# The first half of the first K by the sync queue in fp32, the other half by GpSimd with a cast

## The chip, the cores and the metric

The kernel runs on one core of a Trainium2 chip. The metric is the device time of one execution in microseconds (us). The span of a profile is about 1.85 us shorter than the time of the same execution (before: 424.3 for 426.1). In the profile lines below PE is TensorE (PEld its weight loads), DVE is VectorE, ACT is ScalarE, POOL is GpSimd and SP is the sync engine; a q after the name means its queue. `rk`, `rq` and `rv` are the tiles in SBUF that K, Q and V are loaded to, and `wt` is a place for weights.

## The reference, cut to what matters

Windowed attention over 8 batches, 8 heads, 576 positions, 64 channels; then a Fourier transform along the sequence, 64 modes each multiplied by a complex 512 x 512 weight, the inverse transform, and a residual with a relu layer.

```python
scores = scale * np.matmul(q, k.transpose(0, 1, 3, 2))     # masked to 0 <= i - j < 64, softmax
x = (attn @ v).transpose(0, 2, 1, 3).reshape(B, S, H * D)
X = np.fft.rfft(x, axis=1)
Yr = einsum('bmd,mde->bme', Xr, w_r) - einsum('bmd,mde->bme', Xi, w_i)   # 64 modes
...
return u + np.maximum(u @ w_ch, 0.0)                          # u = x + irfft(Y)
```

The two weight tensors are 64 x 512 x 512 fp32 each, 134 MB together. That is most of what is read.

## The kernel before: the parts that matter

All inputs of the first part and all weights but one (`w_ch`) come by DMAs that GpSimd issues and that cast fp32 to bf16 on the way. Each K, Q or V of one batch is one DMA of 128 partitions x 2 halves x 1152 elements: 1.18 MB read, 0.59 MB written.

```python
    WP = [wlate.tile([128, 2, NC, DM], BF16, name="wt", tag=f"wp{j}") for j in range(LW // 2)]
    ...
    def load(b, which):
        r = raw_tile(which)
        nc.gpsimd.dma_start(
            out=r, in_=RAW[which][b].rearrange("(x g) (p c) d -> (g p) x (c d)", g=4, c=RUN))
        raws[b, which] = r
    ...
    nc.vector.memset(warm, 0.0)
    load(0, "k")
    load(0, "q")
    ...                      # identity; then the tables of the transform (VectorE, ScalarE)
    load(0, "v")
    ...                      # band mask (GpSimd)
    for which in "kqv":
        load(1, which)
```

The places `WP` are for weights that arrive much later; at the start they are empty.

The softmax here doesn't subtract the row's maximum and nothing guards it: scores larger than these inputs give would overflow.

## Time and profile before

| | before |
|---|---|
| median of 3 runs | 425.99 us (425.98 to 426.3) |
| profiled span | 424.3 us |
| busy: PE, VectorE, ScalarE, GpSimd | 82%, 44%, 40%, 19% |
| written by all DMAs | 91.98 MB |
| first packet of the first load | 2.78 us |
| last weight lands | 389.34 us |

PE's 82% looks like the bound, but it is a mean over stages with different limits. What decides is the row of DMA shares by slice, and the end of the chain of waits; the prediction below shows both. A cast load reads two bytes for each byte that it writes, so a row of 213 GB/s written is 426 GB/s read. An uncast fp32 load at full rate shows about 400 to 420 GB/s written. Bear this in mind for every table of stretches.

I use one derived number throughout, the **effective start**: 10 us minus the time that the bytes of the first 10 us need at full rate. At 213 GB/s it is 3.52 us for the kernel before. For bytes that came uncast, half are counted.

### The profile page before, as it was taken

Reading aid. Unit: us, or ns where it says so; the run is one execution under the profiler, and the core shown is the slowest. Engines: PE = TensorE matmul, PEld = TensorE weight load, DVE = VectorE, ACT = ScalarE, POOL = GpSimd, SP = SyncE. Lnnn points to the kernel's source line nnn. Section 1 sums busy time; section 2 is a strip of 40 time slices with the busy share of each in tenths; the row PEclk is TensorE's granted clock in tenths of the full one; section 3 lists DMA queues with packets and bytes.
Section 4 is the critical chain, followed back from the end, with each engine's and each line's share of the span. In section 5 each row is a group of like instructions: output and inputs, shape, how many; then the busy total and the mean of one; then the engine's idle time right before and its main releaser. Section 6 shows DMA issues by size and latency. Waiting matters only on the chain.

```text
span 424.3 us, 8778 instructions
## 1 busy us (share of the span) xinstructions
PE 348.6 (82%) x3762; PEld 217.9 (51%) x3772; DVE 184.6 (44%) x397; ACT 171.3 (40%) x314; POOL 78.9 (19%) x141
## 2 busy tenths in 40 slices
PE   6989998998998899364698977977568986589993
PEld 4655765665665465122365644555234442266782
DVE  5566765766663201061443413332113432140994
ACT  4585765866863311021132312122213332130992
POOL 7231231331121131212111011212121132200000
PEclk9999999999995699755699999999899999979998
DMA  8999999999999999999999999999999999994598
GB/s 143 211 213 213 211 214 213 212 214 211 216 212 215 214 215 263 214 215 214 214 215 214 214 215 214 214 215 213 215 212 214 213 214 214 214 214 92 197 385 328
DMA packets 27782, 91.98 MB, mean 217 GB/s; under 512 B 2352, under 2 KB 2608, under 8 KB 27616
## 3 DMA queue, kind: packets, MB, share of 16 engines
q0 software_dynamic: 24480, 81.80, 96.4%
q1 hardware_dynamic: 3120, 9.50, 5.9%
q8 instruction: 29, 0.48, 0.4%
q10 hardware_dynamic: 144, 0.13, 0.1%
q14 instruction: 9, 0.07, 0.0%
HBM read 162.53 MB, written 9.44 MB: 405 GB/s over the span
## 4 chain that ended last, share of the span: by engine, by line
DMA 44%; PE 36%; DVE 8%; issue 7%; ACT 2%; POOL 1%; DVEq 0%; POOLq 0%
DMA wt<-in_moe_w_r_dram 27%; DMA wt<-in_moe_w_i_dram 17%; PE pso L324 7%; PE pst L226 6%; PE psy L592 5%; PE pso L905 4%; PE psv L243 3%; DVE x_sb L332 3%; PE psx L346 3%; PE pss L381 2%; PE pss L280 2%; PE pss L299 2%; DVE vT L59 2%; DVE ot L928 1%; PE pso L790 1%
## 5 line engine op out<-in xcount | busy, mean ns | idle before, releaser
L592 PE MATMUL psy<-wt,XQ 128*32 128x512 bf16 (+1 forms) x404 | 85.0, 428 | 42.9 <-DMA wt<-in_moe_w_i_dram 27.0
L592 PEld LDWEIGHTS <-XQ 128*32 128x32 bf16 (+1 forms) x476 | 46.8, 133 | 82.3 <-issue 64.9
L621 DVE CAST xT<-pxt 128x256 fp32r<-128x256 bf16 (+1 forms) x68 | 26.0, 435 | 56.3 <-PE pxt L614 40.3
L628 ACT CAST Z<-psz 128x512 fp32r<-128x512 f32 x36 | 21.2, 588 | 58.4 <-PE psz L626 58.1
L305 ACT ACTIVATE et<-pss 128x512 bf16<-128x512 f32 x72 | 39.2, 599 | 13.4 <-PE pss L299 13.4
L626 PE MATMUL psz<-wch,xT 128*128 128x512 f32 x144 | 39.5, 410 | 0.4 <-DVE xT L621 0.4
L324 PE MATMUL pso<-vt,et 128*64 128x65 bf16 (+1 forms) x576 | 34.3, 210 | 4.8 <-DVE x_sb L332 4.7
L324 PEld LDWEIGHTS <-et 128*64 128x64 bf16 (+1 forms) x576 | 24.0, 114 | 17.1 <-issue 9.5
L626 PEld LDWEIGHTS psz<-wch,xT 128*128 128x128 f32 x144 | 25.5, 188 | 11.2 <-issue 5.4
L59 DVE COPY x_sb<-psy 128x256 f32<-128x256 f32 x15 | 6.4, 424 | 53.6 <-PE psy L592 53.5
L58 ACT COPY x_sb<-psy 128x256 f32<-128x256 f32 x15 | 5.6, 374 | 57.8 <-DVE x_sb L59 57.8
L332 DVE TENSOR_TENSOR x_sb<-pso,rcp 128x640 bf16<-128x640 f32 x32 | 26.3, 823 | 0.9
L122 POOL DMA_DIRECT2D wt<-in_moe_w_r_dram x15 | 10.7, 715 | 75.5 <-PE psy L592 68.0
L905 PE MATMUL pso<-Y,trigI 128*128 128x512 f32 x80 | 23.1, 403 | 0.1
L928 DVE TENSOR_TENSOR ot<-pso,x_sb 128x512 f32<-128x512 f32 x35 | 22.2, 685 | 1.5 <-PE pso L905 1.1
L280 PE MATMUL pss<-band,ident_bf 64*64 64x512 bf16 x136 | 20.7, 414 | 1.5 <-ACT et L305 1.5
L59 DVE COPY vT<-pst 128x768 bf16<-128x768 bf16 x16 | 15.3, 958 | 13.0 <-PE pst L226 13.0
L59 DVE CAST x_sb<-psj 128x512 bf16<-128x512 f32 x18 | 12.2, 688 | 19.8 <-PE psj L807 16.6
L117 POOL DMA_DIRECT2D wt<-in_moe_w_r_dram x25 | 13.6, 544 | 35.9 <-PE psy L592 17.2
L910 ACT ACTIVATE pso<-pso 128x512 f32<-128x512 f32 x36 | 19.1, 594 | 0.0
L58 ACT CAST x_sb<-psj 128x512 bf16<-128x512 f32 x18 | 10.6, 586 | 20.5 <-PE psj L807 20.5
L117 POOL DMA_DIRECT2D wt<-in_moe_w_i_dram x21 | 11.4, 542 | 34.1 <-PE psy L592 18.8
(159 smaller groups left out, 533.6 us busy)
## 6 DMA issues: line engine op xcount, KB each, us to landing
wt<-in_moe_w_r_dram POOLq DMA_DIRECT2D x15, 1024.0 KB, 23.0
wt<-in_moe_w_i_dram POOLq DMA_DIRECT2D x15, 1024.0 KB, 25.4
wt<-in_moe_w_r_dram POOLq DMA_DIRECT2D x25, 512.0 KB, 18.0
wt<-in_moe_w_i_dram POOLq DMA_DIRECT2D x21, 512.0 KB, 17.9
out_dram<-ot SPq DMA_DIRECT2D x15, 512.0 KB, 4.3
rk<-in_k_dram POOLq DMA_DIRECT2D x8, 576.0 KB, 9.8
rq<-in_q_dram POOLq DMA_DIRECT2D x8, 576.0 KB, 13.7
rv<-in_v_dram POOLq DMA_DIRECT2D x8, 576.0 KB, 12.4
```

What stands on the lines that cost most here:

```text
L59: return nc.vector.tensor_copy(out=o, in_=i)
L117: nc.gpsimd.dma_start(out=wt, in_=src[m].rearrange("(p c) e -> p c e", c=NC))
L226: nc.tensor.transpose(out=ps[64 * hh:64 * hh + 64, c, :], in_=src[:, hh, (c0 + c) * D:(c0 + c + 1) * D], identity=ident_bf)
L280: nc.tensor.matmul(out=pss[(2 * w + hh) % 3][64 * half:64 * half + 64, :], lhsT=ident_bf[pp, pp], rhs=view(band[pp], 128 * half, [[0, WIN ...
L305: nc.scalar.activation(out=et[:, hh, :], in_=pss[(2 * w + hh) % 3], func=ACT_F.Exp, scale=EX_SCALE)
L324: nc.tensor.matmul(out=pso[po, hh, (i // 2) * VW:(i // 2) * VW + D + 1], lhsT=et[pk, hh, col:col + 64], rhs=vt[pk, 1 - f % 2, 2 * hh + g / ...
L332: nc.vector.tensor_tensor(out=view(x_sb, b * NT * DM + g * D, [[4 * D, 2], [DM, NT], [1, D]]), in0=view(pso, 0, [[512, 2], [VW, NT], [1, D]]),
L592: nc.tensor.matmul(out=psy[r0:r0 + k, :], lhsT=xq(c, m, im, [[NM, k]]), rhs=w[:, c, :], start=(im + c == 0), stop=(im == (m > 0) and c == ...
L621: nc.vector.tensor_copy(out=xT[:, :, w * k:w * k + w], in_=view(psts[k], j, [[128, NC], [n, w]] if n > 1 else [[128, NC], [1, 64], [64, 2]]))
L626: nc.tensor.matmul(out=psz, lhsT=xT[:, c, :], rhs=wch[:, c, :], start=(c == 0), stop=(c == NC - 1))
L905: nc.tensor.matmul(out=tps[n], lhsT=trigI[:, tr:tr + 128], rhs=pair_tile(what, bb), start=False, stop=stop and r0 + k == 128, skip_group_c ...
L928: nc.vector.tensor_tensor(out=ot[:, j], in0=ps, in1=x_sb[:, b, t, :], op=ALU.add)
```

## The change

Its intent is to start the stream of loads earlier: the sync queue has nothing to do before its first DMA (it issues at 0.74 us in the profile after, GpSimd at 1.24). Its half comes without a cast, so it lands in fp32 in an empty weight place, and VectorE casts it.

```diff
     def load(b, which):
         r = raw_tile(which)
-        nc.gpsimd.dma_start(
-            out=r, in_=RAW[which][b].rearrange("(x g) (p c) d -> (g p) x (c d)", g=4, c=RUN))
+        src = RAW[which][b].rearrange("(x g) (p c) d -> (g p) x (c d)", g=4, c=RUN)
         raws[b, which] = r
+        if (b, which) != (0, "k"):
+            nc.gpsimd.dma_start(out=r, in_=src)
+            return
+        wide = view(WP[0], 0, [[1, 2 * RUN * D]]).bitcast(FP32)
+        nc.sync.dma_start(out=wide, in_=src[:, 0])
+        nc.gpsimd.dma_start(out=r[:, 1], in_=src[:, 1])
+        nc.vector.tensor_copy(out=r[:, 0], in_=wide)
```

## The prediction

> **What bounds the kernel now.** I began with the page's 40 slices, because the load, the arithmetic and the store of this kernel overlap and a mean over the span hides which one ends last.
>
> ```profile
> PE   6989998998998899364698977977568986589993
> DMA  8999999999999999999999999999999999994598
> GB/s 143 211 213 213 211 214 213 212 214 211 216 212 215 214 215 263 214 215 214 214 215 214 214 215 214 214 215 213 215 212 214 213 214 214 214 214 92 197 385 328
> ```
>
> One slice is 10.6 us. From the second to the 36th slice the DMA row is a 9 and the rate stays near 213 GB/s (one slice is higher because it carries the one weight that isn't cast to bf16). PE has slices of 3, 4 and 6 in the same time. Only the first slice is short of bytes (143 GB/s). So the loads form one long stream, and what is left after it is the tail in which the result is computed and stored.
>
> The chain that ended last, read at the end of the stream, says the same:
>
> ```profile
> 351.10 18.58 DMA wt<-in_moe_w_i_dram
> ...
> 371.48 17.87 DMA wt<-in_moe_w_i_dram
> 389.34 0.05 issue
> 389.39 0.72 PE psl L796 x16
> ```
>
> The last weight, 512 KB, is issued at 371.48 us and lands at 389.34. At 213 GB/s its own bytes need 0.52 MB / 213 GB/s = 2.5 us, so it spends about 15 us behind earlier loads. The queue is never empty there; GpSimd issues early enough. After the landing follows a tail of 424.3 - 389.3 = 35 us of PE, VectorE and stores that depends on that landing. So the span is: start of the stream, plus its bytes over its rate, plus a fixed tail.
>
> The start of the stream is in the table of stretches (the columns are the stretch, its length, busy time of PE, PEld, DVE, ACT, POOL, then clock, DMA share, GB/s) and in GpSimd's own timeline:
>
> ```profile
> 2.00:2.50 0.50, 0.00 (x0) 0.00 (x0) 0.50 (x1) 0.50 (x1) 0.50 (x2) 1.00 0.00 0
> 2.50:3.00 0.50, 0.00 (x0) 0.00 (x0) 0.07 (x1) 0.00 (x1) 0.50 (x2) 1.00 1.20 65
> 3.00:3.50 0.50, 0.00 (x0) 0.00 (x0) 0.00 (x0) 0.00 (x0) 0.41 (x3) 1.00 0.42 28
> 3.50:4.00 0.50, 0.11 (x1) 0.11 (x1) 0.33 (x2) 0.35 (x2) 0.50 (x3) 1.00 0.81 138
> 4.00:4.50 0.50, 0.50 (x2) 0.41 (x3) 0.49 (x3) 0.50 (x1) 0.49 (x2) 1.00 1.08 207
> ```
> ```profile
> 1.25 0.83 POOL L99 DMA_DIRECT2D rk<-in_k_dram  x1 [0.80 <-POOLq L971]
> 2.07 0.73 POOL L99 DMA_DIRECT2D rq<-in_q_dram  x1
> ```
>
> The first K is issued at 1.25 us, and no byte moves before 2.5 us; a finer look puts the first packet at 2.78, that is 1.5 us after the issue began. Full rate is there from 4.0 us. The first 14 packets alone have a share of 1.196 of 16 engines in half a microsecond: 1.196 x 16 x 0.5 / 14 = 0.68 us each, against about 0.19 us later (1.093 x 16 x 1.0 / 91). So the stream pays a slow first packet on each engine. Over the first 10 us it moved 1.38 MB; at 212 GB/s that is 6.5 us of full rate, so the stream behaves as if it started at full rate at **3.5 us**. That number is all the change can work on, if the above is right.
>
> The arithmetic at the start does not wait for K. The first K lands 5.6 us after its issue, at about 6.85, while PE is in 14 warm-up matmuls until 9.37 and starts the transposes of K at 9.3. So an earlier K by itself starts nothing earlier.
>
> **What the Trainium skill says.** "DMA: Bandwidth & Descriptors", section "Latency and other measured facts", gives a first byte after some 600 ns for the hardware path (sync, scalar) and some 1 us for GpSimd's path. The trace shows longer ones, and a smaller gap: 1.5 us for the first K on GpSimd; on the sync queue, in the tail, a 32 KB transfer issued at 395.35 has its first packet at 396.75 (1.4 us), and the first store, issued at 396.22, starts moving in bulk at about 397.42 (1.2 us). I use 1.2 to 1.4. The same page, section "Issuing engines are not separate DMA queues", says that concurrent issue from several engines saves only the issue time, since all run on the same 16 engines. No view of the kernel before tests that; it is why I count no extra bandwidth. The section "SWDGE vs HWDGE vs iDMA" says that a cast in the DMA is for GpSimd only: hence the fp32 place and VectorE's cast. "VectorE: DVE Perf Modes", section "The perf-mode tier table", has an fp32 copy within SBUF run at two elements a cycle; the trace agrees in slope: the TENSOR_SCALAR of 128x384 fp32 takes 0.36 us and that of 128x256 0.29, so 0.55 ns an element.
>
> **The change part by part.**
>
> *Bytes.* Half of one K goes as fp32 to fp32: 128 x 1152 x 4 = 0.59 MB written in place of 0.29. Does that lengthen the stream? The cast loads write 213 GB/s and so read 426. The stretch 160 to 200 us moved 227 GB/s on average, with the uncast 1.05 MB weight in it: (227 - 214) x 40 us = 0.52 MB more than usual, exactly half of 1.05. So an uncast load writes twice as fast as a cast one, and the engines are limited by what they read. Half a K takes 0.59 / 426 = 1.38 us either way. Cost 0.
>
> *The start.* The sync queue has nothing to do before its first DMA; its only early wait is 0.7 us for the start of the program, and VectorE, released by the same, begins at 0.87. So I put sync's issue at 0.85 and its first packet at 0.85 + 1.2 to 1.4 = 2.05 to 2.25, against 2.78. That is 0.5 to 0.7 us earlier. The slow first packets (0.68 us) then still come, but 0.29 MB x 2 of sync's data, 1.38 us of work, covers the time in which GpSimd's own first packets are slow (2.78 to 3.6), so this loss is paid once and earlier. Effective start about 2.15 + 0.6 = 2.75 in place of 3.5: **a gain of 0.75 us**, from 0.5 to 1.0.
>
> *GpSimd.* Its first issue has 128 rows in place of 256. Loads of 128 rows take it 0.53 to 0.57 us, those of 256 rows 0.70 to 0.83, so about 0.2 us less. The second issue and the identity that PE's warm-up waits for come 0.2 us earlier. PE's warm-up start (3.89) could move by that; it isn't on the path of the stream.
>
> *VectorE.* The cast of 1152 fp32 elements costs 0.36 + 768 x 0.55 ns = 0.78 us. It waits for the sync load, which I expect to land at about 2.15 + 0.6 + 1.4 + 0.5 = 4.6 us. VectorE is in order: between 3.63 and 8.35 it makes the identity and the tables. A wait plus the cast may push the tables' end from 8.35 by 1 to 2 us, and ScalarE's two table steps (8.39 to 8.9) with it, past 9.86, where ScalarE evacuates the first transposes. So PE's attention may begin up to 1 us later. Does it reach the end? Only if the load queue runs dry. Its smallest reserve that I find is at 23.95, where six loads of the first two batches and three more have been issued: 9 x 0.59 MB / 212 GB/s = 25 us from 3.5, so until 28.5: 4.5 us of reserve. 0.75 us earlier and 1 us later still leave 2.8. No cost.
>
> *The weight place* is next written by a load issued at 24.66, long after the cast. No cost.
>
> Sum: -0.75 + 0 + 0 = -0.75 us, that is 425.99 to **425.3** rounded, with the tail unchanged.
>
> **The rivals.** (1) *Hidden anyway*: the sync queue's first packet comes no earlier than GpSimd's, because its first use at the start of a program is slower than in the tail; then the time stays at 426.0. Against it: two tail issues show 1.2 and 1.4 us. For it: no sync DMA is issued early in the trace before, so its start-up is not seen. (2) *VectorE becomes a wait at the start*: the cast stalls the tables, PE starts 1 to 2 us later. If PE set the time in the attention part this would give 427; the load queue's unbroken 213 GB/s speaks against it. (3) *PE sets the attention part and its earlier start by 0.2 us counts too*: 425.0. PE is over 90% busy from 20 to 120 us, which speaks for it, but the weights of the later part must still come through the full stream. (4) *Fp32 packets disturb the cast ones*, both queues sharing 16 engines: some tenths back, 425.7.
>
> **Range and chances.** Rivals 1 and 4 set the upper side, 426.1 with the noise of 0.3 us in the three runs before; an issue at 0.7 and an earlier full rate set the lower side, 424.6. Two per cent is 8.5 us; the whole idle start of the stream is 3.5 us, so faster by that is out of reach, and slower would need the load queue to run dry or an order of instructions that the scheduler spoils later.
>
> **What would show it.** Right: first packet on the sync queue near 2.1, full rate by about 3 us, 10 us mark with some 0.16 MB (bf16 measure) more than before, the last weight landing near 388.6 in place of 389.34, the tail still 35 us. The cast should take about 0.8 us. Wrong: a start of packets at 2.7 or later (rival 1), gaps in the load rate between 20 and 50 us (rival 2), a last landing earlier without an earlier start (rival 3), or a tail of another length, which would be an order or clock effect that I did not foresee.

## The result, and the profile after

| | before | changed |
|---|---|---|
| median, 4 runs each side by side | 426.14 us (425.98 to 426.6) | 426.76 us (426.64 to 427.03) |
| profiled span | 424.3 | 424.8 |
| effective start | 3.52 | 3.78 |
| last weight lands | 389.34 | 389.59 |
| landing to end of span | 35.0 | 35.2 |

The ratio is 1.0014, with an interval from 0.9996 to 1.0031: the same within 2%. The median is above the predicted range and the forecast gain is absent; that the kernel became slower is not clear of the noise, as the interval includes 1.

The page of the changed kernel, by slices of the span, still shows one unbroken stream:

```profile
PE   6999998999988897364598978878569897588993
DMA  8999999999999999999999999999999999994598
GB/s 165 212 212 212 214 214 211 214 212 212 214 214 213 213 214 263 214 214 214 214 215 213 215 215 215 212 215 215 213 214 213 214 214 213 214 212 88 211 378 320
```

Its first slice has 165 GB/s for 143 before, which looks like a gain of 15%. It is not one: the sync half counts double there. Over the first 10 us the changed kernel wrote 162 GB/s, so 1.62 MB. Less half of the uncast 0.59 MB that is 1.325 MB, or 6.22 us of full rate. The effective start is 10 - 6.22 = 3.78 us, 0.26 us **later** than before.

The end of the chain of waits says the same: the last weight lands 0.25 us later than before, and the tail after it goes once through a small load that the kernel before does not have on its chain (the first columns are start and length in us):

```profile
371.30 18.29 DMA wt<-in_moe_w_i_dram
389.59 0.05 issue
389.63 0.73 PE psl L802 x16
...
407.06 4.20 DMA Y<-yl
```

What the two added instructions did is in the timeline (start, length, engine, line, operation, and in brackets the idle time before it and what ended it):

```profile
0.74 0.39 SPq L105 DMA_DIRECT2D wt<-in_k_dram  x1
1.24 0.66 POOL L106 DMA_DIRECT2D rk<-in_k_dram  x1 [0.79 <-POOLq L977]
1.89 0.73 POOL L102 DMA_DIRECT2D rq<-in_q_dram  x1
4.28 0.84 DVE L107 CAST rk<-wt 128x1152 bf16<-128x1152 f32 x1 [1.71 <-DMA wt<-in_k_dram]
9.06 0.42 DVE L159 TENSOR_TENSOR gff<-gff,mtf 128x256 f32<-128x256 f32 x1
```

Sync issues at 0.74, and its first packet starts at 1.77 us, 1.01 us before the first packet of a load in the kernel before. The cast takes 0.84 us; the last step of the tables ends at 9.48 in place of 8.35. So the change does what it was meant to. At 4.0 us the changed kernel has 1.67 us of full rate behind it, the kernel before 0.54: **1.13 us ahead**, counted from the packets.

The loss comes right after. The table of stretches of the changed kernel (stretch, length, busy PE, PEld, DVE, ACT, POOL, clock, DMA share, GB/s):

```profile
2.50:3.00 0.50, 0.00 (x0) 0.00 (x0) 0.07 (x1) 0.00 (x1) 0.48 (x3) 1.00 0.96 350
3.00:3.50 0.50, 0.00 (x0) 0.00 (x0) 0.00 (x0) 0.05 (x1) 0.43 (x4) 1.00 1.04 383
3.50:4.00 0.50, 0.29 (x1) 0.29 (x2) 0.00 (x0) 0.48 (x2) 0.50 (x2) 1.00 0.99 189
4.00:5.00 1.00, 1.00 (x3) 0.82 (x3) 0.72 (x1) 0.96 (x1) 0.99 (x3) 1.00 0.94 141
5.00:6.00 1.00, 1.00 (x4) 0.73 (x3) 0.95 (x6) 0.00 (x0) 0.94 (x5) 1.00 1.01 67
6.00:7.00 1.00, 1.00 (x4) 0.82 (x3) 0.93 (x5) 0.00 (x0) 1.00 (x4) 1.00 0.76 138
7.00:8.00 1.00, 1.00 (x5) 0.86 (x4) 0.97 (x4) 0.51 (x2) 1.00 (x3) 1.00 1.12 212
```

and of the kernel before in the last four of these:

```profile
4.00:5.00 1.00, 1.00 (x3) 0.82 (x4) 0.99 (x5) 1.00 (x1) 0.99 (x4) 1.00 1.09 210
5.00:6.00 1.00, 1.00 (x4) 0.81 (x3) 0.93 (x4) 0.14 (x1) 0.94 (x3) 1.00 1.10 210
6.00:7.00 1.00, 1.00 (x3) 0.76 (x3) 0.49 (x4) 0.62 (x2) 1.00 (x5) 1.00 1.11 210
7.00:8.00 1.00, 1.00 (x4) 0.77 (x3) 0.92 (x5) 0.00 (x0) 1.00 (x2) 1.00 1.13 217
```

From 4 to 8 us the changed kernel wrote 141 + 67 + 138 + 212 = 558 KB of cast data, which is 2.62 us of full rate in 4 us: it **lost 1.38 us** there, the kernel before 0.03. The DMA share (a packet counts whole where it begins) is near 1 even where only 67 GB/s moved, so the packets there are slow rather than missing: of the packets that began between 5 and 6 us, 14 took over 0.4 us, up to 1.9 us, where 0.19 us is usual. In order of start they are among the 90th to the 122nd of GpSimd's packets. Its half of K has 128, so they lie about where the 16 engines pass from K to Q; which load each one belongs to the trace does not say. I call this the hole. It turns the lead of 1.13 us at 4 us into an arrears of 0.26 us at 10 us, which then stays (0.27 at 380 us).

### The profile page after: what moved, and what is told of

It is laid out like the page before. It is cut to its first block, busy times and chain, and to the rows that moved or that the text cites. A ratio compares the mean times of both kernels' runs of the same rounds, so it can differ in the third digit from the quotient of the medians.

```text
span 424.8 us, 8781 instructions
## 1 busy us (share of the span) xinstructions
PE 347.7 (82%) x3762; PEld 216.9 (51%) x3772; DVE 185.4 (44%) x398; ACT 171.2 (40%) x314; POOL 78.8 (19%) x141
## 4 chain that ended last, share of the span: by engine, by line
DMA 37%; PE 36%; issue 12%; DVE 9%; POOL 2%; ACT 2%; POOLq 0%; DVEq 0%; SPq 0%
DMA wt<-in_moe_w_r_dram 23%; DMA wt<-in_moe_w_i_dram 14%; PE pso L330 7%; PE pst L232 6%; PE psy L598 4%; PE psv L249 3%; DVE x_sb L338 3%; PE psw L751 3%; PE pso L911 3%; PE pss L387 2%; PE pss L286 2%; PE psx L352 2%; DVE ot L934 2%; PE pss L305 2%; DVE vT L59 2%
## 5 line engine op out<-in xcount | busy, mean ns | idle before, releaser
L598 PE MATMUL psy<-wt,XQ 128*32 128x512 bf16 (+1 forms) x404 | 86.1, 426 | 42.9 <-DMA wt<-in_moe_w_i_dram 26.0
```

The source lines that it names most:

```text
L598: nc.tensor.matmul(out=psy[r0:r0 + k, :], lhsT=xq(c, m, im, [[NM, k]]), rhs=w[:, c, :], start=(im + c == 0), stop=(im == (m > 0) and c == ...
```

## The experiments

Each is measured by the same three numbers: the loss in 4 to 8 us, the lead over the kernel before at 10 us (how much earlier the effective start is), and the landing of the last weight. The rows are grouped as the argument goes. Each row is one profile; two pairs of the same kernel show how far two profiles differ: 1.38 and 1.11 lost (changed and e13), 0.37 and 0.21 (e6 and e12).

| run | GpSimd's first packet, us | sync's last packet ends | loss 4-8 us | lead at 10 us | last weight lands |
|---|---|---|---|---|---|
| before | 2.78 | - | 0.03 | 0 | 389.34 |
| changed | 3.42 | 3.91 | 1.38 | -0.26 | 389.59 |
| e13 (changed, again) | 3.27 | 3.88 | 1.11 | -0.09 | (1) |
| e1 no cast | 3.40 | 3.89 | 1.31 | -0.18 | 389.9 |
| e5 cast late | 3.38 | 3.82 | 0.97 | +0.24 | 389.7 |
| e7 no cast, no tables | 3.31 | 3.75 | 0.94 | +0.10 | (2) |
| e4 whole K + unread sync half | 3.48 | 3.92 | 1.43 | -0.44 | 391.8 |
| e3 two halves, GpSimd only | 2.58 | - | 0.88 | -0.38 | 389.9 |
| e8 Q in halves, GpSimd only | 2.79 | - | 0.07 | +0.07 | 389.1 |
| e10 Q issued later | 3.56 | 4.01 | 0.77 | +0.28 | 389.5 |
| e11 half K, Q, half K, GpSimd | 2.60 | - | 0.29 | +0.08 | (2) |
| e9 Q first on GpSimd | 3.59 | 4.07 | 0.48 | +0.48 | 388.9 |
| e14 sync reads V | 3.62 | 4.29 | 1.07 | -0.17 | 390.0 |
| e15 as e4, sync reads V | 3.98 | 4.37 | 1.17 | -0.34 | 391.9 |
| e18 sync half in two transfers | 3.23 | 6.33 | 0.57 | +0.24 | (2) |
| e6 K by sync | 4.70 | 5.10 | 0.37 | +1.12 | 388.3 |
| e12 K by sync, again | 4.99 | 5.41 | 0.21 | +1.02 | 388.7 |
| e16 Q by sync | 4.98 | 5.54 | 0.30 | +1.03 | 388.5 |
| e19 Q by sync, V early | 5.00 | 5.41 | 0.20 | +1.08 | 388.3 |
| e17 changed + second sync load | 5.11 | 5.66 | 0.05 | +1.00 | (1) |

In e4, e15 and e17 the lead counts bytes that nobody reads, worth 1.38 us; without them e17 is 0.38 us behind. (1) In these profiles the granted clock was 0.911 and 0.915, and PE, not the load, closed the chain; see e13. (2) e7, e11 and e18 lost 2 to 5 us of stream between 100 and 380 us for a reason that I did not find; only their first 10 us are used.

### Is it VectorE's cast, or its late tables? e1, e5, e7

The first theory was a lock. The Trainium skill, page "SBUF — State Buffer", section "SBUF: two separate sides", says that an fp32 copy within SBUF on VectorE shuts GpSimd out of a shared pair of ports, so that GpSimd can't write the descriptors of its DMAs. The trace of the changed kernel has such a sign: a band step on GpSimd took 0.78 us beside the cast (from 4.43 us), the same step in the kernel before 0.26.

e1 removes the cast (the half is set to zero; a wrong K):

```diff
-        nc.vector.tensor_copy(out=r[:, 0], in_=wide)
+        nc.vector.memset(r[:, 0], 0.0)
```

> Wrong on purpose: half of the first K is zeros set at the start, the sync load into the weight place stays, the VectorE cast is gone. Theory A (the cast is what breaks the load stream between 4 and 7 us, by shutting GpSimd out while it runs): the rate from 4 to 7 us goes back to about 210 GB/s from 141, 67 and 138; some 1 us more of the stream is done by 10 us; last weight lands near 388.4 to 388.7; time 425.2 to 425.6. Theory B (GpSimd's queue pays its slow first packets again because it starts behind the sync queue's packets, cast or not): the hole stays, 425.9 to 426.9.

Measured: 426.93 us, ratio 1.0017 [1.0005, 1.0029]. The hole is there without the cast:

```profile
4.00:5.00 1.00, 1.00 (x3) 0.82 (x3) 0.96 (x5) 0.95 (x1) 0.99 (x5) 1.00 1.06 152
5.00:6.00 1.00, 1.00 (x4) 0.73 (x3) 0.96 (x4) 0.15 (x1) 0.94 (x3) 1.00 1.09 74
6.00:7.00 1.00, 1.00 (x4) 0.82 (x3) 0.47 (x3) 0.47 (x2) 1.00 (x4) 1.00 0.81 145
```

e5 keeps the cast but holds it back until the tables are done:

```diff
-        nc.vector.tensor_copy(out=r[:, 0], in_=wide)
+        casts.append(lambda: nc.vector.tensor_copy(out=r[:, 0], in_=wide))
...                                  # VectorE's order held as written
+    casts.pop()()                   # after gen_trig
```

> As the changed kernel, with the cast held back on VectorE until after the tables (about 8.4 us instead of 4.3). A: the hole between 4 and 7 us is gone; if the cast as such does the harm, a hole shows up after 8.4 us instead, and if it only hurts while descriptors of the first loads are being fetched, none does; 425.2 to 425.7 in the second case. B: hole at 4 to 7 us as in the changed kernel, 426 to 427. The first K transposes start near 9.2 to 9.5 in both.

Measured: 427.42 us, ratio 1.0021 [1.0009, 1.0033]; 88 GB/s in 5 to 6 us, loss 0.97.

e7 takes away the cast and the tables (wrong, relative error 0.027):

```diff
-        for t0, t1 in ((0, 3), (3, NT)):
-            ...
-            gen_trig(tmp, mt, n * NM, ...)
+        nc.vector.memset(trigF, 0.0)
```

> Wrong on purpose: as e1_no_cast, and VectorE's and ScalarE's cosine and sine tables are replaced by zeros set at the start, so VectorE does almost nothing between 3 and 9 us. Theory Q (VectorE's fp32 work in that time keeps GpSimd from writing the descriptors of the loads that it has already issued): no hole at 5 to 6 us, rate near 210 GB/s, about 1 us more moved by 10 us than in e1_no_cast. P and R: the hole stays as in e1_no_cast, 74 GB/s from 5 to 6 us.

Measured: one look, 429.33 us at a clock of 0.905, so the time says nothing. VectorE was busy for 0.65 us of the 4 us in question, and the loss was still 0.94 us. What follows: the cast did cost GpSimd half a microsecond of its own work, but neither the cast nor VectorE's tables make the hole. Its size varies by some tenths between executions (e13 below: 1.11 for 1.38), so the differences among 0.94, 0.97 and 1.31 are not read. A second sign comes from e17 below: there the same cast ran beside a band step of 0.85 us, and there was no hole. e5 also shows how loosely the start and the time hang together: 0.24 us ahead at 10 us, its last weight landed 0.3 us late.

### Is it the sync queue, or the halves? e3, e4, e8

e3 does without sync and without a cast: two GpSimd loads of 128 rows.

```diff
-        nc.sync.dma_start(out=wide, in_=src[:, 0])
+        nc.gpsimd.dma_start(out=r[:, 0], in_=src[:, 0])
         nc.gpsimd.dma_start(out=r[:, 1], in_=src[:, 1])
-        nc.vector.tensor_copy(out=r[:, 0], in_=wide)
```

> No sync load and no cast: GpSimd loads the two halves of the first K as two DMAs of 128 rows. A and B: stream like the kernel before (full rate from 4 us, no hole), 426.0 plus or minus 0.3. Rival C (a load of half a K, 128 rows, is itself what starts slowly): packets of 0.5 us and more after the first ones, and a hole as in the changed kernel, 426.5 or more.

Measured: 426.37 us, ratio 1.0005 [0.9992, 1.0019]. A loss of 0.88 us, mostly at 6 to 7 us (99 GB/s). The two halves have 256 packets, and the slow ones (0.7 us and more) are mostly the 262nd to the 285th, where Q begins. So a hole of this kind needs no sync load.

e4 leaves GpSimd's loads as before and adds the sync load, which nobody reads:

```diff
-        nc.gpsimd.dma_start(out=r[:, 1], in_=src[:, 1])
-        nc.vector.tensor_copy(out=r[:, 0], in_=wide)
+        nc.gpsimd.dma_start(out=r, in_=src)
```

> GpSimd loads the whole first K as before, and the sync queue loads half of it once more into the weight place, where nobody reads it; no cast. 0.59 MB more to read, 1.38 us at 426 GB/s. A: no hole; the stream starts 1.1 us earlier and carries 1.4 us more, so about +0.3 us against before, 426.2 to 426.6. B: hole behind the sync packets, another 1 us on top, 427.0 to 427.6.

Measured: 428.85 us, ratio 1.0061 [1.0049, 1.0073]; loss 1.43, last weight at 391.8. So the hole does not need the halves either: a sync load beside the unchanged GpSimd loads is enough. Of the 2.45 us by which the last weight came later, 1.38 are the extra bytes. Nor is the hole tied to the start of Q: the packets of 0.9 us and more in e4 are among the 50th to the 85th of the 256 of the whole K.

e8 is the kernel before with the first Q, not K, in two GpSimd loads:

```diff
+        if (b, which) != (0, "q"):
+            nc.gpsimd.dma_start(out=r, in_=src)
+            return
+        for x in range(2):
+            nc.gpsimd.dma_start(out=r[:, x], in_=src[:, x])
```

> The kernel before with Q, not K, loaded as two GpSimd DMAs of 128 rows; K whole as before. P and Q: engines come to Q at 6.2 us, more than 3 us after its issue, so no slow packets, full rate as before. C (a load of 128 rows makes the load after it start slowly, as the halves of K did in e3_halves_gpsimd): first packets of 1 us at the start of the second half of Q or of V, a hole of some tenths between 7.5 and 10 us.

Measured: one look, 426.13 us, no hole (loss 0.07). Loads of 128 rows as such are harmless. Its span also goes through the wait for `yl` in the tail, so that wait needs no sync load.

### Is it the time between GpSimd's issue and its first packets? e9, e10, e11

Another theory (P in the expectations) was that a GpSimd load is not ready until some microseconds after its issue, and that Q was wanted too soon. e9 issues Q ahead of the half K, e10 issues Q after the small constants (at 2.74 us in place of 1.89), and e11 uses GpSimd only, with half K, Q, half K.

```diff
e9:  -        nc.gpsimd.dma_start(out=r[:, 1], in_=src[:, 1])
     +        casts.append(lambda: nc.gpsimd.dma_start(out=r[:, 1], in_=src[:, 1]))
      ...     load(0, "q")
     +    casts.pop()()
e10: -    load(0, "q")             # after load(0, "k")
     +    load(0, "q")             # just before load(0, "v")
e11: -        nc.sync.dma_start(out=wide, in_=src[:, 0])
     -        nc.gpsimd.dma_start(out=r[:, 1], in_=src[:, 1])
     -        nc.vector.tensor_copy(out=r[:, 0], in_=wide)
     +        nc.gpsimd.dma_start(out=r[:, 0], in_=src[:, 0])
     +        casts.append(lambda: nc.gpsimd.dma_start(out=r[:, 1], in_=src[:, 1]))
      ...     load(0, "q")
     +    casts.pop()()
```

> The changed kernel with GpSimd issuing Q before its half of K, all else the same. P: engines come to Q at 3.5 us, 1.5 us after its issue ended, so they are slow there as the first packets of the kernel before are (0.6 to 1.1 us each), then the half of K is long ready: a loss of about 0.5 in place of 1.3 us, about 0.5 us ahead of before at 10 us, 425.5 to 425.9. R: as the changed kernel or e4_extra_sync, slow packets from 4 to 7 us, 426.5 to 427.

> The changed kernel with one line moved: GpSimd issues Q after its small constants, ending at about 3.3 us in place of 2.6; the engines still finish the half of K at about 5.0. P (the engines wait at Q because its load was issued too short a time ago): the slow first packets of Q last 0.7 us longer, to about 6.5 to 7.8 us instead of 5.8 to 7.1, and some 0.5 us less has been moved by 8 us than in the changed kernel (4.28 us' worth there, about 3.8 here). If the hole ends at a fixed time or belongs to the order of loads, it stays at 4.3 us' worth by 8 us.

> GpSimd alone, no sync load, no cast: half of K, then Q, then the other half of K. The engines come to Q at about 4.4 us, some 1.9 us after its issue ended. P: first packets of Q of 1 us and more from 4.4 us on, ending near 6 us, and none when the engines come to the second half of K near 8 us. If a start behind another queue or the cast were needed for slow packets, none here.

Measured: e9 427.52 us, ratio 1.0016 [0.9987, 1.0045], with a profile that is 0.48 us ahead and whose last weight lands at 388.9; its timed runs scatter from 425.97 to 428.19 and don't confirm a gain. e10 one look, 426.55; its loss is smaller (0.77, spread as 168, 164, 180 and 177 GB/s over the four microseconds), though Q had less time. e11 one look, 430.12 (see (2) above), loss 0.29, with Q in use 1.9 us after its issue. The profile of e9 came out as P said (0.48 lost, 0.48 ahead), those of e10 and e11 against it: less time did not hurt. A comparison of e15 and e16 (below) speaks against it too. In both GpSimd issues the whole K at 1.25 us; among K's packets that began between 6 and 7 us, nine took 0.4 to 0.88 us in e15, and none over 0.31 us in e16. A fixed time from issue to readiness does not give that, so this theory falls.

### All of the first K by sync: e6, e12

```diff
-        nc.sync.dma_start(out=wide, in_=src[:, 0])
-        nc.gpsimd.dma_start(out=r[:, 1], in_=src[:, 1])
-        nc.vector.tensor_copy(out=r[:, 0], in_=wide)
+        for x in range(2):
+            wide = view(WP[x], 0, [[1, 2 * RUN * D]]).bitcast(FP32)
+            nc.sync.dma_start(out=wide, in_=src[:, x])
+            nc.vector.tensor_copy(out=r[:, x], in_=wide)
```

> The whole first K by the sync queue in fp32 into two weight places, two VectorE casts; GpSimd begins with Q at 1.25 us, so Q's load has been issued 3.4 us before the engines can come to it (about 4.6). Theory P (a GpSimd load issued at the start is not ready for the DMA engines until some 3 to 4 us after its issue ended, and engines that come to it sooner have first packets of 1 us and more): no hole, 1.1 us ahead of before at 10 us, 425.0 to 425.5. Theory R (packets of GpSimd's queue are slow whenever they follow those of the sync queue): slow packets from 4.6 on, no gain left, 426 to 427.

> e6_k_by_sync once more, beside the changed kernel on the same chip, for the time: 1.1 us ahead by 10 us as before, last weight near 388.3; 0.6 us faster than before and 1.2 us faster than the changed kernel if the gain of the stream reaches the end, equal to before if it doesn't.

Measured: 425.38 us, ratio 0.9979 [0.995, 1.0008], and again, on another chip, 425.51 us, ratio 0.9981 [0.9965, 0.9996]. At 10 us the stream is 1.12 and 1.02 us ahead; its last weight lands 1.1 and 0.6 us earlier. The medians are 0.60 and 0.56 us under the kernel before, though e6's interval still includes 1. This is what the prediction wanted to see, with two halves in place of one. The rates of e12, the smaller lead of the two, show no such hole:

```profile
4.00:5.00 1.00, 1.00 (x3) 0.77 (x3) 0.61 (x1) 0.41 (x1) 0.94 (x4) 1.00 1.07 419
5.00:6.00 1.00, 1.00 (x4) 0.79 (x3) 0.38 (x2) 0.00 (x0) 1.00 (x5) 1.00 1.04 189
6.00:7.00 1.00, 1.00 (x4) 0.82 (x3) 0.95 (x4) 0.00 (x0) 1.00 (x2) 1.00 1.10 207
7.00:8.00 1.00, 1.00 (x3) 0.76 (x3) 0.97 (x5) 0.00 (x0) 1.00 (x2) 1.00 1.12 210
```

e13 is the changed kernel once more, on the chip of e12 (no edit):

> The changed kernel itself, once more: does the hole come back with the same size (rates near 141, 67, 138 GB/s from 4 to 7 us, 0.2 to 0.3 us behind before at 10 us), and is the time again 0.4 to 0.7 us over before? If the hole is a chance of one profile, the rates differ.

Measured: 427.12 us, ratio 1.0014 [0.9995, 1.0032]; loss 1.11. The loss comes back, if smaller and in another shape: 118, 150, 166 and 182 GB/s from 4 to 8 us, without the 67 of the first profile. Its profile also shows where scatter of the times comes from. The granted clock was 0.911, and the chain of waits near its end is no longer a DMA:

```profile
351.01 19.20 DMA wt<-in_moe_w_i_dram
376.95 0.55 PE psl L802 x16
...
390.83 0.53 PE psl L802 x16
```

In this profile PE is late at the end of the stream, and an earlier landing would be worth less there. The slowest runs of the kernel before tend to such clocks (428.91 us at 0.915, 429.74 at 0.911), though not all: 428.41 came at 0.927. Tenths of a microsecond can't be read from single times here.

### One K on two queues, or any sync load? e14, e15, e16

Two theories were left. R: two pieces of one tensor in flight slow each other. B: any sync load beside GpSimd's first load does. e14 is the changed kernel, and e15 is e4, with the sync load from another tensor; e16 gives the whole first Q to sync and the whole first K to GpSimd.

```diff
e14, e15:
+        far = RAW["v"][B - 1].rearrange("(x g) (p c) d -> (g p) x (c d)", g=4, c=RUN)
-        nc.sync.dma_start(out=wide, in_=src[:, 0])
+        nc.sync.dma_start(out=wide, in_=far[:, 0])
e16: the loop of e6, under
+        if (b, which) != (0, "q"):
```

> The changed kernel, but the sync queue's half comes from the last V (another tensor, as large); half of the first K is wrong on purpose. Theory R (pieces of one K in flight together slow each other): the loss of stream between 4 and 8 us falls from 1.1-1.4 us to under 0.4, and the lead over the kernel before stays near +0.9 us at 10 us. Theory B (any sync load beside the first GpSimd load slows it): loss stays at 1.0 us or more, with under 160 GB/s in 5 to 6 us.

> As e4_extra_sync (GpSimd loads the whole K, sync an extra half that nobody reads), but the extra half comes from the last V. e4 lost 1.43 us between 4 and 8. R: under 0.4 lost, last weight about 0.3 us later than before at most (1.38 us more to read, 1.1 us earlier start). B: 1.0 us or more lost and the last weight near 391 us, as in e4.

> GpSimd loads the whole first K; the sync queue loads the first Q in two fp32 halves, cast by VectorE. R: no split tensor is on both queues, but Q's halves are on one; loss under 0.5 us between 4 and 8, stream ahead of before by about 0.9 us at 10 us, time about 425.5. B: loss of 1.0 us or more and time 426 or above.

Measured: e14 427.04 and e15 428.96 (one look each), losses 1.07 and 1.17: R falls. e16 425.38 us, ratio 0.9963 [0.9927, 1.0], loss 0.30 and 1.03 us ahead: B in that wide form falls too, because e16 has a sync load beside GpSimd's first load. The end of e16's chain of waits:

```profile
369.74 18.72 DMA wt<-in_moe_w_i_dram
388.51 0.73 PE psl L799 x16
```

Between e15 and e16 GpSimd's first load is the same, the whole K at 1.25 us. In their loads up to 3 us two things differ: sync carries 0.59 or 1.18 MB, and GpSimd's second load is queued at 2.07 or 2.93 us.

### How long must the sync queue have work? e17, e18, e19

e17 leaves everything of the changed kernel in place and adds a second sync load, which nobody reads. e18 cuts the one sync load into two. e19 is e16 with the next GpSimd load issued at once.

```diff
e17: +        far = RAW["v"][B - 1].rearrange("(x g) (p c) d -> (g p) x (c d)", g=4, c=RUN)
     +        nc.sync.dma_start(out=view(WP[1], 0, [[1, 2 * RUN * D]]).bitcast(FP32), in_=far[:, 0])
e18: -        nc.sync.dma_start(out=wide, in_=src[:, 0])
     +        for p0 in (0, 64):
     +            nc.sync.dma_start(out=wide[p0:p0 + 64], in_=src[p0:p0 + 64, 0])
e19: load(0, "v") moved up to follow load(0, "q")
```

> The changed kernel with a second sync load of the same size (0.59 MB, first half of the last V, read by nobody) right after the first. S (the sync queue's work covers GpSimd's slow early stage if it lasts to about 5 us): under 0.4 us of full rate lost between 4 and 8 us, extra bytes counted. T (two transfers): the same. N (two GpSimd loads queued early): 1.0 us or more lost, with 5 to 7 us at under 160 GB/s.

> The changed kernel with its one sync transfer cut into two of 64 rows; the same bytes. S: as in the changed kernel, 0.9 us or more lost between 4 and 8 us. T: under 0.4 us. N: 0.9 us or more.

> e16 (first Q by sync in two halves, whole first K by GpSimd) with GpSimd's next load, the first V, issued right after K at about 2.1 us in place of 2.93. N: 0.8 us or more lost between 4 and 8 us. S and T: under 0.4 us, as in e16 (0.3).

Measured (one look each): 427.44, 427.1 and 425.27 us. e17 has no hole at all:

```profile
4.00:5.00 1.00, 1.00 (x3) 0.82 (x3) 0.38 (x1) 0.95 (x1) 0.99 (x4) 1.00 1.01 419
5.00:6.00 1.00, 1.00 (x3) 0.73 (x3) 0.95 (x4) 0.00 (x0) 0.94 (x4) 1.00 1.10 254
6.00:7.00 1.00, 1.00 (x4) 0.82 (x3) 0.97 (x5) 0.00 (x0) 1.00 (x4) 1.00 1.10 205
7.00:8.00 1.00, 1.00 (x4) 0.82 (x3) 0.96 (x4) 0.20 (x1) 1.00 (x2) 1.00 1.12 214
```

Its GpSimd issues are those of the changed kernel to the hundredth (1.24, 1.89, 3.47 us). Sync's work lasts to 5.66 in place of 3.91 us, and GpSimd's packets start at 5.11 in place of 3.42 (the cast starts at 4.62 in place of 4.28). In the first microsecond after that start e17 has 84 GpSimd packets of 192 ns on average, the changed kernel 53 of 266, then 56 of 305 and 38 of 283. e19 keeps its lead too (loss 0.20), so a second early GpSimd load does no harm behind enough sync work. e18 falls between the stated limits (0.57), and its sync packets started only at 2.14 and trailed to 6.33; it separates nothing cleanly.

What follows: in these runs a sync load of **0.59 MB** beside GpSimd's first loads left a slow stage of GpSimd's queue after it (0.5 to 1.4 us lost), and 1.18 MB in two transfers left at most 0.4 us. e17 is the direct test of it, in one profile; its difference to the changed kernel, 1.1 to 1.3 us, is well above the 0.3 us between two profiles of one kernel.

What stays open is what the slow packets wait for. The trace tells neither when descriptors are written nor what an engine does between packets, and e3 shows a hole without sync while the kernel before, with GpSimd's packets from 2.78 us on, has none. e17 can't tell whether more bytes or a second full-size transfer is the remedy, nor whether it helps only because GpSimd's packets then start later (at 4.7 us or after in all five runs with 1.18 MB).

## Why the prediction was wrong, by its steps

- **The bound was right.** The span is the start of the stream plus its bytes plus a tail. In the runs without a hole (e6, e12, e16, e19) 1.0 to 1.1 us of lead at 10 us became 0.6 to 1.1 us at the last landing. The carry-over is not exact: e10 was 0.28 ahead at 10 us and e5 0.24, and their last weights landed 0.2 and 0.3 us late. Such misses are as large as the change's own net loss at 10 us, so this loss is not shown to be the whole reason for 426.76 in place of 426.14; that the forecast gain was used up is.
- **Sync's start was right in direction and more than right in size.** Issue at 0.74 (stated 0.85), first packet at 1.77 (2.05 to 2.25). Rival 1 is refuted.
- **Bytes: right.** The stretches from 2.5 to 3.5 us moved 350 and 383 GB/s, and a longer uncast load 419 (e17), against 426 stated.
- **The step that failed** is "this loss is paid once and earlier", with its 1.38 us of sync data that "covers the time in which GpSimd's own first packets are slow". I took the length of that slow time, 2.78 to 3.6 us, from the kernel before and held it fixed. With sync's packets ahead, GpSimd's first packet moved from 2.78 to 3.42 us, and its slow time then ran to about 7 us. The term was to be a gain of 0.75 us; up to 4 us it was 1.13, and then the hole took 1.38 where the kernel before lost 0.03. Net, the effective start came 0.26 us later (0.09 in the repeat, e13).
- **Rival 4 came nearest, with the wrong size:** "some tenths back", 425.7. It was over a microsecond. That fp32 packets disturb the cast ones is not shown to be the reason: sync's last packet ended at 3.91 us, before most of the hole, and e3 has a hole without any fp32 packet. It was also the one rival against which I had no measured number. Rival 3, an earlier attention, did not show: landing and time came later, not earlier.
- **GpSimd's issue, right:** 0.66 us in place of 0.83, and the second issue 0.18 us earlier.
- **VectorE: right.** Cast 0.84 us (0.78 stated), start 4.28 (4.6), tables' end 1.13 us later (1 to 2). e1, without the cast, is no faster. Rival 2 is refuted.
- **The tail** was to be unchanged and was 0.3 us longer, with a wait for the small `yl` load on its chain. e8 has this wait and a tail of 35.2 us without any sync load, e4 has a sync load, no such wait and a tail of 34.9, so it is not shown to come from the change. Landing and tail together make the 0.5 us between the two profiled spans; the 0.62 us between the medians lies within the noise of that.
- **A slip in the sum:** 425.99 - 0.75 is 425.24, so the centre should have read 425.2, not 425.3.

The class (same within 2%) was right, the time and the range were not. A version that does gain is the one with the whole first K, or the whole first Q, on sync: 425.4 to 425.5 us, ratios 0.9963 to 0.9981 with intervals that reach 1.0008 (e6), 0.9996 (e12) and 1.0 (e16), within 2% all the same. e12 was 1.6 us under e13, of which some may be e13's lower clock.

## What to carry to other kernels

A slow start that you measured in one kernel is not a constant that you can hide behind something else; putting another queue's packets ahead of it can lengthen it, so look at the rate for several microseconds after the join of two queues and not only at the first packet. When an early transfer is meant to cover another queue's start, try twice the size before giving it up: here one half of K lost the gain and two halves kept it. And compare bytes in one measure (here what was read), because the first slice's GB/s rose by 15% while the stream fell behind.

## What the Trainium skill lacked or had wrong

- "DMA: Bandwidth & Descriptors", section "Latency and other measured facts", has a first byte after some 600 ns on the hardware path and some 1 us on GpSimd's. Here the first load of the program took 1.03 us on sync (0.74 to 1.77) and 1.53 us on GpSimd (1.25 to 2.78). The gap agrees roughly, both values are longer.
- The same page, section "Issuing engines are not separate DMA queues", counts concurrent issue as a saving of issue time only. That does not contradict the runs: the lead of e16 (1.03 us at 10 us) is about what sync's first packet came earlier (1.01 us). What is lacking is the loss: the changed kernel was 0.26 us behind, with 1.38 us lost between 4 and 8 us. No page says that GpSimd's first loads can run at a third of their rate (67 for 210 GB/s) after a short sync load.
- "SBUF — State Buffer", section "SBUF: two separate sides": a stalled GpSimd beside an fp32 copy is seen (0.78 for 0.26 us), but without the copy the loads were as slow (e1: 74 GB/s from 5 to 6 us), and with it e17 lost only 0.05 us, so it isn't what slows them.
